# Attention and feed-forward on one core: loads held back longer near a range's end, x sums one step later, and the last half product moved ahead and stored as whole rows

## The chip, the cores and the metric

The kernel runs on one core of one Trainium2 chip. The metric is the device time of one execution in microseconds, lower is better. Three runs of the kernel before the change took 386.1, 386.33 and 386.3 us; the median is 386.3.

## What is computed

The reference is a softmax attention over 8 batches, 12 heads, 448 positions and 64 elements per head, followed by a feed-forward layer on all 3584 tokens:

```python
scores = scale * np.matmul(q, k.transpose(0, 1, 3, 2))
scores = scores - np.max(scores, axis=-1, keepdims=True)
attn = np.exp(scores)
attn = attn / (np.sum(attn, axis=-1, keepdims=True) + 1e-09)
x = np.matmul(attn, v)            # (8, 12, 448, 64) -> (3584, 768)
...
h = x @ w_in                      # (3584, 768) @ (768, 2048)
g = np.maximum(0.01 * h, h)
out = g @ w_out                   # (3584, 2048) @ (2048, 768), float32
```

## The kernel before

**Two streams of work.** The attention works in *units* of two heads of one batch: 8 x 6 = 48 units. A unit's scores (L316, L319) go to PSUM, ScalarE takes their exponential (L328, L331, L333), `rows` (L983) multiplies the exponentials by v (L340, L347), divides by the row sums (L999, L1000) into a tile `x`, and `x_transposes` (L376) turns that tile into `xT` by a DMA transposition that SP issues (L271). A transposition of q and k into `qkT` (L280, `dma_transposes`) is issued by SP too.

The feed-forward runs over seven *ranges* of tokens (`cuts`, L41: 640, 512, 512, 512, 512, 384 and 512 tokens), here called range 0 to 6. For each range `hidden(i)` (L530) computes h = leaky(x w_in), and `second(i)` (L1157) computes g w_out, in two pairs of 128-row blocks (`block_pair`, L664; range 0 has a plain pair first). In the time of `second(i)` PE's matmuls are interleaved with the attention of the units that the next range needs: `place` (L1094) decides from a small model of time (`model["now"]`, in microseconds) when a burst of scores, a `rows` or a tail is put between two quarter products.

**Seven products for eight.** Both matrix products save multiplications: a product of 2 x 2 blocks is done with seven half products and some sums of blocks. The sums of x that `hidden(i+1)` needs are made on VectorE by `mix_x_part` (L489, its instruction is L502), from `xT`: four sums for the first two thirds of the depth (`slice(0, 2)`) and four for the last third. The first four read what the last but one unit of a range wrote, the others what its last unit wrote. In `second`, the list `fresh` holds from which model time on each of the two lots may be emitted: 5.0 after the unit's `rows`, and from then on one sum per step. VectorE executes in the order of emission, so a sum that waits for its transposition holds up all that stands behind it.

In `block_pair`, `early` computes four products into PSUM banks `a` and `b` and `late` the last ones; each is copied (`keep`, L691) or added (`join`, L697) to an output tile on VectorE before its bank is used again. `deep_sums` (L615, instruction L625) prepares one product of the second pair that is itself split into seven (`deep`, L628, matmuls L649, additions L653), which runs beside the next `hidden`.

**Loads.** `advance` (L957) is called every few steps and emits at most one cast of q and k, one cast of v (both on GpSimd, L186 to L199) and, if its argument `calm` is true, one load (`load_soft`, L149, issued by GpSimd, L159) of q, k or v of two units. GpSimd executes these in the order of emission. In `second`, `calm` is true until all but one of the units that the next range needs have had their `rows`, and again once all x sums are emitted; in `hidden` it is always true.

**The end.** The last pair has no next `hidden` beside which its deep product could run, so `block_pair` with `last` runs `early`, the steps of `deep` between them, and then `closing` (L732). There the output tiles are `o1` and `o2` (in the profile `e`), and stores go to SP's and ScalarE's queues (`both`). `closing` computes, in this order: the fourth product in two quarter-width pieces, with the sixth step of `deep` between them; the fifth product (`s3`, `t3`, eight matmuls of 384 columns) into bank `b`; a join of its right half (L744) and a store of the right half of `o2`; the left half of `o2`, for which the first quarter is a copy by ScalarE (L746) and the second an addition (L747); the seventh and last step of `deep`, four L649 matmuls of 192 columns, added to the first quarter; a store of the left half; and the last two pieces of `o1`, each added (L754) and stored. A store of 128 rows is cut in two where the rows cross a boundary of 112: here 16 rows on SP's queue and 112 on ScalarE's for `o2`, 48 and 80 for `o1`.

Of the kernel before, what the change touches and what calls it, by code (L numbers as in the profile page):

```python
# [16 lines left out]
def kernel(  # L17
# [372 lines left out]
    def store(o, t0, cols=slice(0, DM), queues=(nc.sync, nc.sync)):  # L390

        queues = list(queues)
        done = 0
        while done < P:
            b, j = divmod(t0 + done, S)
            so, p = divmod(j, SC)
            n = min(SC - p, P - done)
            dst = out[b * S:(b + 1) * S].rearrange("(p so) n -> so p n", so=NSC)
            queues.pop(0).dma_start(out=dst[so, p:p + n, cols], in_=o[done:done + n, cols])
            done += n  # L400
# [227 lines left out]
    def deep(i):  # L628

        one, two = (ts(x[1], P) for x in spots(i)[1])  # L630
        lo, hi = slice(MH, MH + QH), slice(MH + QH, MD)
        s3, s1 = h_mix[:, :QH, 0], h_mix[:, QH:, 0]
        t, (t2, t3, t4) = w_mix[:, 2], (deep_mix[:, x] for x in range(3))
        left, right = slice(0, QW), slice(QW, NW)
        o = [kept[i, c] for c in range(2)]
        end = i + 1 == NR
        taken = [slots.pop(0) for _ in range(2 if end else 1)]
        b, a = (x[:, 0, :QW] for x in taken) if end else (taken[0][:, x, :QW] for x in range(2))
        for ps, first, x, w, c, cols in (
            (b, True, h[:, lo, one], t[:, :QH, left], 0, left),  # L640
            (a, True, h[:, hi, one], t[:, QH:, left], 0, left),
            (b, False, s1, t2, 0, right),
            (a, True, h[:, lo, two], t[:, :QH, right], 1, right),
            (b, False, s3, t3, 1, right),
            (a, False, h[:, hi, one], t[:, QH:, right], 0, right),
            (b, False, h[:, hi, two], t4, 1, left),
        ):
            for m in range(QH):
                nc.tensor.matmul(ps, x[:, m], w[:, m], start=(first and m == 0), stop=(m == QH - 1), skip_group_check=True)  # L649
            if end and c and ps is a:  # L650
                nc.scalar.copy(o[c][:, cols], ps)
            else:
                nc.vector.tensor_add(o[c][:, cols], o[c][:, cols], ps)  # L653
            if ps is a and first and c == 0:
                nc.vector.tensor_sub(h[:, hi, one], h[:, hi, one], s1)
            if ps is a and not first:
                store(o[0], token(i, spots(i)[1][0][1]), slice(0, NW) if end else slice(0, DM))
            if w is t4:
                if not end:
                    store(o[1], token(i, spots(i)[1][1][1]))  # L660
                slots.extend(taken)
            yield

    def block_pair(i, c):  # L664

        lo, hi = slice(0, MH), slice(MH, MD)
        x1, x2 = spots(i)[1][c]
        one, two = ts(x1, P), ts(x2, P)
        s3 = h_mix[:, :, c]
        t2, t3, t4 = (w_mix[:, x] for x in range(3))  # L670
        t1 = w_out_sb[:, lo, NW:]
        left, right = slice(0, NW), slice(NW, DM)
        if i + 1 == NR and c:
            o1, o2 = (e_all[:, x, :2 * DM].bitcast(F32) for x in range(2))
        else:
            o1, o2 = (o_pool.tile([P, DM], F32, name="o") for _ in range(2))
        kept[i, c] = o2
        b, a = banks
        t0 = token(i, x2)
        last = t0 + P == B * S  # L680

        def product(ps, x, w, first=False, cols=slice(0, NW)):
            for m in range(MH):
                if m in (2, 4, 6):
                    yield
                nc.tensor.matmul(  # L686
                    ps[:, cols], x[:, m], w[:, m], start=(first and m == 0), stop=(m == MH - 1), skip_group_check=True,
                )

        def keep(o, at, ps, by=nc.vector.tensor_copy):  # L690
            by(o[:, at], ps[:, :NW])  # L691

        idle = nc.scalar.copy
        calm = idle if i + 1 == NR else nc.vector.tensor_copy

        def join(o, at, ps):
            nc.vector.tensor_add(o[:, at], o[:, at], ps[:, :NW])  # L697

        def early():
            yield from product(b, h[:, lo, one], w_out_sb[:, lo, left], first=True)  # L700
            nc.vector.tensor_sub(h[:, lo, one], h[:, lo, two], h[:, lo, one])
            short = cuts[i + 1] - cuts[i] < 4 * P
            keep(o1, left, b, idle if c == 0 and short else calm)
            yield
            yield from product(a, h[:, hi, one], w_out_sb[:, hi, left], first=True)
            join(o1, left, a)
            if last:
                store(o1, token(i, x1), left)
            nc.vector.tensor_sub(h[:, hi, one], h[:, hi, one], h[:, lo, one])
            yield  # L710
            yield from product(b, h[:, lo, one], t2)
            keep(o1, right, b, calm)
            yield
            if last:
                return
            yield from product(a, h[:, lo, two], t1, first=True)
            keep(o2, right, a, calm)
            yield

        def late():  # L720
            yield from product(b, s3, t3)
            if i:
                keep(o2, left, b, calm)
            join(o2, right, b)
            if i + 1 == NR:
                store(o2, t0, right)
            yield
            yield from product(a, h[:, hi, one], w_out_sb[:, hi, right])
            join(o1, right, a)
            store(o1, token(i, x1))  # L730

        def closing(more):  # L732

            both = (nc.sync, nc.scalar)
            pieces = [(ps, ts(x, QW), slice(NW + x * QW, NW + (x + 1) * QW)) for x, ps in enumerate((a, slots[0][:, 0]))]
            for ps, cols, at in pieces:
                yield from product(ps, h[:, lo, two], t1[:, :, cols], first=True, cols=cols)
                idle(o2[:, at], ps[:, cols])
                if ps is a:
                    yield  # L740
                    next(more)
                yield
            yield from product(b, s3, t3)
            join(o2, right, b)  # L744
            store(o2, t0, right, both)
            idle(o2[:, :QW], b[:, :QW])  # L746
            nc.vector.tensor_add(o2[:, QW:NW], o2[:, QW:NW], b[:, QW:NW])  # L747
            yield
            for _ in more:
                yield  # L750
            store(o2, t0, left, both)
            for x, (ps, cols, at) in enumerate(pieces):
                yield from product(ps, h[:, hi, one], w_out_sb[:, hi, right][:, :, cols], cols=cols)
                nc.vector.tensor_add(o1[:, at], o1[:, at], ps[:, cols])  # L754
                store(o1, token(i, x1), at, both)
                if not x:
                    yield

        yield
        if last:  # L760
            more = deep(i)
            for x, _ in enumerate(early()):
                if x in (0, 4):
                    next(parts[0])
                yield
                if x > 2 and x % 2:
                    next(more)
                    yield
            yield from closing(more)
            return  # L770
        if not c:
            parts[:] = [deep_sums(i)]
        for x, _ in enumerate(early()):
            if i and c and x in (9, 13):
                next(parts[0])
            yield
        for x, _ in enumerate(late()):
            if i and not c and x == 4:
                next(parts[0])
            yield  # L780
        if i:
            return
        yield
        yield from product(b, h[:, hi, two], t4)
        keep(o2, left, b)
        store(o2, t0)
        banks.reverse()
# [369 lines left out]
    def second(i):  # L1157
# [5 lines left out]
        for c in range(len(spots(i)[1])):  # L1163
            whole = c < plain(i)
            for x, _ in enumerate((plain_pair if whole else block_pair)(i, c)):
                fine = 1 if whole else 2
                if x % (2 * fine) == 0:
                    advance(all(summed) or rows_done < need[i + 2] - 1)
                if c or x:
                    model["now"] += 0.65 / fine  # L1170
                if c == 0 and x > 2 and x % 2:
# [10 lines left out]
                    next(deeps, None)  # L1182
                for y in range(2):
                    if fresh[y] is None and i + 1 < NR and rows_done >= need[i + 2] - 1 + y:
                        fresh[y] = model["now"] + 5.0
                for y, todo in enumerate(x_sums if x % fine == 0 else ()):
                    if fresh[y] is not None and fresh[y] <= model["now"] and not summed[y]:
                        summed[y] = next(todo, 0) is not None
# [72 lines left out]
```

## Time and profile before

| what | value |
|---|---|
| median of three runs | 386.3 us |
| the profiled execution | 385.61 us |
| its span, first to last instruction | 383.8 us |
| PE busy | 371.3 us (97%) |
| DVE busy | 248.6 us (65%) |
| ACT busy | 260.5 us (68%) |
| POOL busy | 187.8 us (49%) |
| mean granted TensorE clock | 0.999 |
| DMA, mean over the span | 125 GB/s |

Times within the kernel are counted from the start of the span. PE, PEld, DVE, ACT, POOL and SP are TensorE's matmuls, its weight loads, VectorE, ScalarE, GpSimd and SyncE. In a timeline a row gives the start, the duration, the engine, the line of the kernel, the operation, what is written and read, the number of instructions merged into the row and, in brackets, how long the engine had been idle before and what ended that. The rows marked SPq and ACTq are the queues that issue DMAs. In the view of waits a row gives who waited for whom, the total, the number of times and the longest. The view of DMA issues gives a size and the median time from issue to landing. PE is busy nearly all the time, so the rows to look at are those in which it waits, and the tail after its last matmul, at 379 us.

### The profile page before, as it was taken

To read this page: it belongs to the slowest core of one execution; us is meant where nothing else is said; L and a number is where in the kernel's file an instruction comes from. 1 tells how busy PE (TensorE), PEld (TensorE's weight loads), DVE (VectorE), ACT (ScalarE), POOL (GpSimd) and SP (SyncE) were. 2 spreads that over 40 slices of the span, in tenths; PEclk is the share of its full clock that TensorE was granted. 3 is DMA by queue.
4 is the path that set the end of the run, shared out by engine and by line. 5 is a ranking of instruction groups with operands and counts; after the bars stand their busy time and mean duration, and the time that the engine had idled before them with its cause. 6 is when DMAs were issued, how large, how long until landed. Compare 5 with 4: busy or idle time off the path is not lost.

```text
span 383.8 us, 10136 instructions
## 1 busy us (share of the span) xinstructions
PE 371.3 (97%) x4024; PEld 266.3 (69%) x4024; DVE 248.6 (65%) x550; ACT 260.5 (68%) x400; POOL 187.8 (49%) x376
## 2 busy tenths in 40 slices
PE   7899999999999999999999999999999999999994
PEld 3565557766698565996559966589665995679764
DVE  5763848456866857666676575766847775685752
ACT  6988885765768785658756688657687568536621
POOL 8997731987969355526566255761637020000000
PEclk9999999999999999999999999999999999999999
DMA  9999999899999469948599484896637530322023
GB/s 158 196 199 203 183 204 172 109 166 208 145 201 112 73 128 126 144 116 109 111 124 160 116 111 79 119 174 138 91 76 132 111 108 0 79 56 61 23 76 91
DMA packets 99456, 47.85 MB, mean 125 GB/s; under 512 B 63696, under 2 KB 96208, under 8 KB 99408
## 3 DMA queue, kind: packets, MB, share of 16 engines
q0 software_dynamic: 40384, 22.47, 46.6%
q1 hardware_dynamic: 58576, 24.27, 30.4%
q8 instruction: 31, 0.51, 0.6%
q10 hardware_dynamic: 448, 0.47, 0.4%
q14 instruction: 17, 0.14, 0.1%
HBM read 45.61 MB, written 11.01 MB: 148 GB/s over the span
## 4 chain that ended last, share of the span: by engine, by line
PE 85%; DMA 7%; DVE 4%; issue 1%; ACT 1%; POOL 1%; ACTq 0%; DVEq 0%; POOLq 0%
PE g L686 22%; PE g L555 14%; PE sc L555 14%; PE sc L347 5%; PE sc L319 5%; DMA xT<-x 5%; PE g L421 4%; PE sc L316 4%; PE sc L649 4%; PE sc L359 3%; PE g L800 3%; PE g L841 2%; PE sc L340 2%; DMA w_in_mix<-in_k_dram 2%; PE g L359 1%
## 5 line engine op out<-in xcount | busy, mean ns | idle before, releaser
L328 ACT ACTIVATE e<-sc 128x896 bf16<-128x896 f32 (+1 forms) x144 | 123.5, 921 | 33.5 <-PE sc L319 20.1
L686 PE MATMUL g<-w_out_sb,h 128*128 128x384 bf16 (+1 forms) x416 | 78.7, 324 | 2.2 <-DVE o L691 2.2
L686 PEld LDWEIGHTS <-h 128*128 128x128 bf16 x544 | 50.3, 98 | 39.8 <-issue 11.9
L544 ACT ACTIVATE h<-c 128x512 bf16<-128x512 f32 (+1 forms) x72 | 43.6, 611 | 30.1 <-DVE c L570 12.8
L555 PEld LDWEIGHTS <-w_in_sb 128*128 128x128 bf16 x576 | 54.6, 98 | 7.0 <-issue 1.5
L186 POOL COPY qkb<-fq 112x512 bf16<-112x512 bf16 x36 | 24.3, 676 | 62.2 <-DMA qkT<-qkb 42.7
L555 PEld LDWEIGHTS <-w_in_mix 128*128 128x128 bf16 x432 | 40.5, 98 | 3.7
L999 DVE RECIPROCAL rec<-sc 112x8 f32<-112x8 f32 x42 | 8.7, 207 | 42.5 <-PE sc L347 18.6
L197 POOL COPY v<-fv 128x384 bf16<-128x384 bf16 x30 | 15.4, 512 | 42.0 <-PE sc L347 25.4
L347 PE MATMUL sc<-v,e 128*128 128x65 bf16 x720 | 33.3, 194 | 0.0
L319 PE MATMUL sc<-qkT 64*128 64x448 bf16 (+1 forms) x210 | 32.8, 353 | 0.0
L347 PEld LDWEIGHTS <-e 128*128 128x128 bf16 x720 | 31.2, 98 | 1.3
L1000 DVE TENSOR_TENSOR x<-sc,rec 112x512 bf16<-112x512 f32 x42 | 29.0, 692 | 1.5
L691 DVE COPY o<-g 128x384 f32<-128x384 f32 x43 | 23.8, 553 | 8.7 <-PE g L686 8.6
L555 PE MATMUL g<-xT,w_in_sb 128*128 128x256 bf16 (+1 forms) x216 | 28.5, 268 | 0.8 <-DVE o L697 0.8
L555 PE MATMUL sc<-xT,w_in_sb 128*128 128x256 bf16 (+1 forms) x216 | 28.5, 268 | 0.0
L653 DVE TENSOR_TENSOR o<-o,sc 128x192 f32<-128x192 f32 x39 | 13.7, 351 | 20.3 <-PE sc L649 20.3
L340 PE MATMUL sc<-v,e 128*128 128x130 bf16 x120 | 26.5, 221 | 0.0
L697 DVE TENSOR_TENSOR o<-o,g 128x384 f32<-128x384 f32 x36 | 19.8, 550 | 8.6 <-PE g L686 4.9
L190 POOL COPY qkb<-fk 128x384 bf16<-128x384 bf16 x30 | 19.6, 653 | 7.1 <-DMA fk<-in_k_dram 7.1
L159 POOL DMA_DIRECT2D fv<-in_v_dram x33 | 20.6, 630 | 4.1 <-POOL v L199 2.4
L567 ACT COPY c<-g 128x512 f32<-128x512 f32 (+1 forms) x12 | 6.8, 567 | 22.5 <-PE g L555 22.0
(151 smaller groups left out, 766.8 us busy)
## 6 DMA issues: line engine op xcount, KB each, us to landing
fq<-in_q_dram POOLq DMA_DIRECT2D x18, 224.0 KB, 5.4
w_in_sb<-in_moe_w_in_dram POOLq DMA_DIRECT2D x4, 768.0 KB, 11.3
w_out_sb<-in_moe_w_out_dram POOLq DMA_DIRECT2D x4, 768.0 KB, 17.7
out_dram<-o SPq DMA_DIRECT2D x7, 336.0 KB, 3.3
out_dram<-o SPq DMA_DIRECT2D x7, 288.0 KB, 2.7
fk<-in_k_dram POOLq DMA_DIRECT2D x15, 128.0 KB, 5.1
fv<-in_v_dram POOLq DMA_DIRECT2D x15, 128.0 KB, 3.7
out_dram<-o SPq DMA_DIRECT2D x7, 240.0 KB, 2.8
```

Of the source, the lines that this page charges most:

```text
L159: nc.gpsimd.dma_start(out=t[p, :n, :, :so].rearrange("p u h so d -> p (u h) (so d)"), in_=(q, k, v)[x][b, hs, keys].rearrange("h (p so) d ...
L186: by(t[:SC, x].rearrange("p so h d -> p h so d"), f)
L319: nc.tensor.matmul(ps[:, j, :S].rearrange("p (so s) -> p so s", so=NSC), t[p, 1, c], t[p, 0, :, :SC], start=True, stop=True,)
L328: nc.scalar.activation(e[:, :, c, :], ps[:n, :, :S], AX.Exp, scale=scale)
L340: nc.tensor.matmul(ps, e[:, EM + qc * SC:EM + qc * SC + P], vt[:, 2 * KC:].rearrange("p j d -> p (j d)"), start=True, stop=False, skip_gro ...
L347: nc.tensor.matmul(ps[:, j * (D + 1):(j + 1) * (D + 1)], e[:, at:at + P], vt[:, j * KC + c], start=False, stop=(c == KC - 1), skip_group_c ...
L544: nc.scalar.activation(hs[:, m:m + 2, cols], x.rearrange("p (m t) -> p m t", m=2), AX.Prelu, alpha=0.01)
L555: nc.tensor.matmul(ps[:, j * nh:(j + 1) * nh], w[:, kk, ts(j, P)], x[:, kk], start=(first and j == 0 and kk == 0), stop=(kk == KH - 1), sk ...
L686: nc.tensor.matmul(ps[:, cols], x[:, m], w[:, m], start=(first and m == 0), stop=(m == MH - 1), skip_group_check=True,)
L691: by(o[:, at], ps[:, :NW])
L697: nc.vector.tensor_add(o[:, at], o[:, at], ps[:, :NW])
L1000: nc.vector.tensor_mul(x, ps[:, :, :, :D], rec.to_broadcast([SC, 2, 2 * NP, D]))
```

## The change

Three things are changed.

1. In `second`, the loads are withheld from `rows_done >= need[i + 2] - 2` on, one unit earlier than before, until all x sums of the next range are emitted.
2. The x sums may be emitted 6.0 model microseconds after their unit's `rows`, not 5.0.
3. In `closing`, the seventh step of `deep` is made ahead of the fifth product, right behind the second piece of the fourth product. `deep` copies it (ScalarE) into the first quarter of `o2` instead of adding it. The fifth product is then joined to the right half and to the left half by two VectorE additions of 384 columns, and `o2` is stored as whole rows.

```diff
@@ deep
-            if end and c and ps is a:
+            if end and c and (ps is a or cols is left):
                 nc.scalar.copy(o[c][:, cols], ps)
             else:
                 nc.vector.tensor_add(o[c][:, cols], o[c][:, cols], ps)
@@ closing
             for ps, cols, at in pieces:
                 yield from product(ps, h[:, lo, two], t1[:, :, cols], first=True, cols=cols)
                 idle(o2[:, at], ps[:, cols])
-                if ps is a:
-                    yield
-                    next(more)
+                yield
+                next(more)
                 yield
             yield from product(b, s3, t3)
             join(o2, right, b)
-            store(o2, t0, right, both)
-            idle(o2[:, :QW], b[:, :QW])
-            nc.vector.tensor_add(o2[:, QW:NW], o2[:, QW:NW], b[:, QW:NW])
-            yield
+            join(o2, left, b)
+            store(o2, t0, queues=both)
             for _ in more:
-                yield
-            store(o2, t0, left, both)
+                pass
+            yield
@@ second
-                    advance(all(summed) or rows_done < need[i + 2] - 1)
+                    advance(all(summed) or rows_done < need[i + 2] - 2)
...
-                        fresh[y] = model["now"] + 5.0
+                        fresh[y] = model["now"] + 6.0
```

More of the change, by code (lines that the diff above doesn't have):

```diff
@@ L744, in closing @@
             join(o2, right, b)
-            store(o2, t0, right, both)
-            idle(o2[:, :QW], b[:, :QW])
-            nc.vector.tensor_add(o2[:, QW:NW], o2[:, QW:NW], b[:, QW:NW])
+            join(o2, left, b)
+            store(o2, t0, queues=both)
+            for _ in more:
+                pass
             yield
-            for _ in more:
-                yield
-            store(o2, t0, left, both)
             for x, (ps, cols, at) in enumerate(pieces):
```

## The prediction

> **What bounds the kernel now.** I read the page first: PE is busy for 371.3 of 383.8 us, at a granted clock of 0.999, so time can only be won where PE stands still or after its last matmul. The view of waits, for PE over the whole span, says where it stands still (total, times, longest):
>
> ```profile
> PE g L686 <- DVE o L691: 2.2, 3, 0.9
> ...
> PE g L555 <- DVE o L697: 0.8, 3, 0.3
> ```
>
> All other PE waits lie in the first 59 us, which the change does not reach. These six come in three pairs, at the ends of ranges 1, 2 and 3 (near 149, 199 and 249 us). The timeline of the first shows what holds DVE up:
>
> ```profile
> 141.03 1.23 POOL L159 DMA_DIRECT2D fv<-in_v_dram  x2 [0.30 <-POOL v L199]
> ...
> 141.49 5.11 SPq L271 DMA_TRANSPOSE xT<-x  x2
> ...
> 147.62 1.46 PE L686 MATMUL g<-w_mix,hmix 128*128 128x384 bf16 x8
> ...
> 148.12 0.43 DVE L502 TENSOR_TENSOR x_mix<-xT 128x512 bf16<-128x512 bf16 x1 [1.94 <-DMA xT<-x]
> ...
> 149.14 0.55 DVE L691 COPY o<-g 128x384 f32<-128x384 f32 x1
> ...
> 149.74 1.46 PE L686 MATMUL g<-w_out_sb,h 128*128 128x384 bf16 x8 [0.66 <-DVE o L691]
> ...
> 151.46 0.82 PE L555 MATMUL g<-xT,w_in_sb 128*128 128x256 bf16 x6 [0.26 <-DVE o L697]
> ```
>
> The first x sum (L502) stands in DVE's order ahead of the copy (L691) that frees PE's bank. It waits for the transposition issued at 141.49, which lands 6.54 us later (the chain's row for it), and a v load issued at 141.03 runs beside that transposition. The end of range 4 shows the same three products with DVE in time:
>
> ```profile
> 295.85 1.46 PE L686 MATMUL g<-w_mix,hmix 128*128 128x384 bf16 x8
> ...
> 297.15 1.46 PE L686 MATMUL g<-w_out_sb,h 128*128 128x384 bf16 x8
> ...
> 298.45 0.66 PE L555 MATMUL g<-xT,w_in_sb 128*128 128x192 bf16 x6
> ```
>
> From the hmix product to the first hidden product that is 298.45 - 295.85 = 2.60 us. At the three places it is 151.46 - 147.62 = 3.84, 200.78 - 196.94 = 3.84 and 250.37 - 246.26 = 4.11. The excess, 1.24 + 1.24 + 1.51 = **3.99 us**, is what can be won; the waits show only 3.0, since each modelled matmul end holds 0.15 us of pipeline after the next could start.
>
> **Loads held back.** By the built order PE, SP and ACT keep their instructions up to the last pair; only POOL's L159 loads move. At the ends of ranges 1 to 4 it is the v load alone that moves (two DMAs, 1.23 us of POOL), from ahead of two v casts and one q/k cast to behind them. At the end of range 0 a v, a q and a k load move behind three casts (the v load behind four). The transposition so loses its neighbour. What it takes alone: the one issued at 137.57 landed at 139.95, the one at 325.48 at 327.81, 2.4 and 2.3 us; the rows of L271 give 2.3/3.0/6.8 as least, median and most. At 141.49 two output stores (issued 140.20 and 140.79) are ahead of it on SP's queue, whose packets run until 142.9 in the trace, so I take 142.9 plus its 0.6 us of packets plus 0.5 to 2 us to complete (both occur): it lands at 144.0 to 145.5. DVE reaches the sum at about 146.6, so the wait goes, with 1 us to spare.
>
> **x sums a step later.** The model's 5.0 becomes 6.0: at the ends of ranges 1 to 3 the first x sum goes behind the last deep sum (L625, 0.42), and each later one moves one place behind a copy or join. DVE then runs, with the 0.46 to 0.47 us from start to start that these rows show: L691 at 147.82 (the t1 product ends at 147.78), x sums at 148.29 and 148.75, L691 at 149.2, L697 at 149.67 to 150.21. PE starts its next product at 148.93 without a wait and the first hidden product at 150.27, against 147.62 + 2.60 = 150.22. So 0.05 stays at each place: 3.99 - 0.15 = **3.8 us won**. What is late next: four part-2 sums (0.28 each) end at about 152.2, while the third hidden product, which needs them, starts at 153.3; they are hidden by PE's four products before it. At the end of range 5 one more 0.43 us sum falls behind the joins, and L570 starts 0.43 later than 342.81; its bank is next wanted at 344.79, so it costs nothing (0.4 at most without that cover).
>
> **What the late loads cost.** The v load comes behind the casts, at about 145.3, and its packets (1.8 us after issue in this trace) from 147.1, when those of the second transposition (issued 145.41) are through. It then shares with three qkT transpositions that are first used in the next second half, near 174. The q and k loads behind it land 2 to 3 us later and the casts with them; POOL stood idle for 5.19 us before the next v cast (166.86, waiting for PE), which hides it. At range 0 the first q/k cast moves from 112.5 to about 118, and its transposition is issued at 128.59 after waiting for PE. Cost: nothing.
>
> The Trainium skill's DMA: Bandwidth & Descriptors, Rules for kernel authors, speaks against this part: to overlap transfers with compute it says to issue the DMA early. By that rule late loads would reach PE; the idle rows of POOL above say there is room, and the rival below has its price.
>
> **The last pair.** The end of the kernel reads so:
>
> ```profile
> 375.86 1.46 PE L686 MATMUL g<-w_mix,hmix 128*128 128x384 bf16 x8
> ...
> 377.43 0.56 DVE L697 TENSOR_TENSOR e<-e,g 128x384 f32<-128x384 f32 x1 [1.68 <-PE g L686]
> ...
> 378.02 0.39 ACTq L399 DMA_DIRECT2D out_dram<-e  x1
> ...
> 378.45 0.32 ACT L746 COPY e<-g 128x192 f32<-128x192 f32 x1 [2.07 <-DVE e L697]
> 378.80 0.35 DVE L747 TENSOR_TENSOR e<-e,g 128x192 f32<-128x192 f32 x1 [0.81 <-ACT e L746]
> ...
> 379.45 1.33 ACTq L399 DMA_DIRECT2D out_dram<-e  x3
> ```
>
> PE's work is the same, but the four L649 matmuls (0.33 us) now go ahead of the fifth product: its join starts at 377.43 + 0.33 = 377.76, the second join (0.55) at 378.23, done at 378.78. A DVE add at L747 and one at L653 (0.35 each) go, an L697 comes; ACT's copy L746 becomes L651, early and hidden. The whole-row stores are issued at 378.81, where the left ones went at 379.45, and ACT's two 80-row stores follow at 379.25 and 379.70 instead of 379.93 and 380.40. The issues are 0.70 us earlier. Against it stands that the right half, 196 KB, which left at 378.02 while the queues were empty, now waits until 378.81. Bounds: -0.70 if issue sets the last landing (2.15 us after issue, as before); and if data does, the page's median of 3.3 us for a 336 KB store gives 378.81 + 3.3 = 382.1, and 196 KB more at the 215 to 305 GB/s of the last stretch 0.65 to 0.9, so 382.75 to 383.0 against the last landing at 382.55: up to +0.4. The 3.3 has loads beside it, so I take **-0.2**.
>
> The same page of the Trainium skill, Anatomy of one DMA, fits 2.0 us plus bytes at 436 GB/s; the 336 KB piece would then be an estimated 2.8 us and the last 60 KB one 2.1, so the end would come 0.7 earlier and the sum would be -4.5. The packets of the whole-row store issued near 369.6 run from 370.6 to 372.2, 393 KB in 1.6 us or 245 GB/s, and I keep mine.
>
> **Sum.** -3.8 - 0.2 = -4.0 us. The profiled execution (385.61 us, of which the span is 383.8) would take 381.6; it lies 0.69 below the median of the runs, so the median 386.3 becomes **382.3**. With 4.0 + 0.7 at best, and 3.5 and +0.4 at worst, this case spans 381.6 to 383.2.
>
> **Rivals.**
> 1. *The transposition lands as late as before*, since the stores ahead of it or an instruction fetch hold it and not the load. For it: a 16 KB fetch lies beside it at 143.5, and the one issued at 335.56 took 4.25 us with no load. Against: with loads beside it it took 5.3 to 6.8 at all four places. Then only the order acts: x sum at 148.12, L691 148.58, two sums, L691 149.95, L697 150.42 to 150.97, hidden product 151.02 instead of 151.46. That is 0.44 x 3 + 0.2 = 1.5: 384.8.
> 2. *The wait moves to the second transposition*, which meets the deferred load instead. It bites when that lands over 6.8 us after its issue (145.41 + 6.8 = 152.2, less than 1 us of sums before 153.3). At 8 us it takes 1.2 back at each of three places: 382.3 + 3.6 = 385.9.
> 3. *Slower: loads too late.* At the end of range 0 three loads go at about 106.5 and the casts behind them must be done by 128.59, 134.93 and 138.86, when SP wants to issue the qkT transpositions in order. The page's landing times for q, k and v are 5.4, 5.1 and 3.7 us; it decides from about 11 us a load, and at the 16 us of the slowest v row (at the start) the third cast is some 7 us late, which PE pays at once: 386.3 - 4.0 + 7 = 389.3.
> 4. *The change does not do what it says*: the built order shows that it does; what remains is that a wait elsewhere takes the time, 386.
>
> **Chances.** Forecast 0.73, rival 1 0.12, rival 2 0.05, rival 3 0.06, rival 4 0.04. The range 381.4 to 384.8 takes in the forecast's span, most of rival 1 and little else. A measurement can tell about 0.2% (0.8 us) from no change: faster 0.86 (the forecast, rival 1, a little of rival 2), same 0.07, slower 0.07.
>
> **What would show it.** Right: no PE wait on L691 or L697 at the three places, 2.6 us from the hmix product to L555, transpositions of the last row but one landing within 4 us, the range ends 1.2, 2.4 and 3.8 us earlier, joins at 377.8 and 378.2 less 3.8. Wrong: an x sum that still waits for xT; POOL casts that wait so long for fq or fk that SP's qkT issues move; a last landing over 3.8 us after the whole-row issue.

## The result, and the profile after

| kernel | median of its runs | ratio to the kernel before, with 95% interval | profiled execution | its span |
|---|---|---|---|---|
| before | 386.2 us (8 runs) | 1 | 385.61 us | 383.8 us |
| changed | 383.01 us (8 runs) | 0.9933 (0.991 to 0.9956) | 382.95 us | 381.1 us |

The changed kernel is 0.44 to 0.9% faster. 382.3 was forecast, with a range of 381.4 to 384.8. The view of waits for PE, over the whole span of the changed kernel, no longer has L691 or L697. After the first 59 us only one wait is left, and it is new, 0.2 us on L653:

```profile
PE g L236 <- DVE gate L231: 1.2, 1, 1.2
...
PE sc L649 <- DVE o L653: 0.2, 1, 0.2
```

The timeline of the changed kernel at the end of range 1 answers to the one shown of before:

```profile
141.83 5.12 SPq L271 DMA_TRANSPOSE xT<-x  x2
...
146.78 0.42 DVE L502 TENSOR_TENSOR x_mix<-xT 128x512 bf16<-128x512 bf16 x1
...
147.96 1.46 PE L686 MATMUL g<-w_mix,hmix 128*128 128x384 bf16 x8
147.98 1.23 POOL L159 DMA_DIRECT2D fv<-in_v_dram  x2
148.16 0.56 DVE L691 COPY o<-g 128x384 f32<-128x384 f32 x1 [0.96 <-PE g L686]
...
150.56 0.82 PE L555 MATMUL g<-xT,w_in_sb 128*128 128x256 bf16 x6
```

The x sum at 146.78 has no bracket: it waits for nothing. The v load stands 6.2 us behind the transposition instead of 0.5 ahead of it. DVE now waits for PE (L691, 0.96), where PE had waited for DVE, and from the hmix product to the hidden product it is 150.56 - 147.96 = 2.60 us.

The same stretch and two others can be read off the two traces. Where the 2.7 us of the spans come from:

| stretch | before | changed | difference |
|---|---|---|---|
| start to the first hidden product of range 1 | 104.43 | 104.78 | +0.35 |
| hmix product to hidden product, ends of ranges 1, 2, 3 | 3.84, 3.84, 4.11 | 2.60, 2.60, 2.60 | -3.99 |
| the same, ends of ranges 4 and 5 | 2.60, 2.60 | 2.60, 2.60 | 0 |
| first hidden product of range 6 to the end of the last matmul | 38.78 | 39.19 | +0.41 |
| end of the last matmul to the last landing | 3.57 | 4.22 | +0.65 |
| last landing to the end of the span | 1.29 | 1.19 | -0.10 |

The sum is -2.68. The first row is chance: in the executions of this study that stretch took 104.4 to 107 us, also in kernels with the same instructions there (105.11 with the last pair alone changed, 104.43 in the kernel before). Two rows gave back a quarter of what was won. The end of the changed kernel, in its timeline:

```profile
372.96 1.46 PE L686 MATMUL g<-w_mix,hmix 128*128 128x384 bf16 x8
373.16 0.32 ACT L651 COPY e<-sc 128x192 f32<-128x192 f32 x1
...
374.53 1.02 DVE L697 TENSOR_TENSOR e<-e,g 128x384 f32<-128x384 f32 x2 [2.00 <-PE g L686]
...
375.57 1.75 SPq L399 DMA_DIRECT2D out_dram<-e  x3
375.58 1.76 ACTq L399 DMA_DIRECT2D out_dram<-e  x3
```

The order is as forecast, and so is the time of issue: the whole-row stores go 0.16 us before the end of the last matmul (375.74), where the left ones went 0.48 behind it. But the view of DMA issues (window 374 to 381) shows what they then take. The columns are number, size of each and median time to landing:

```profile
out_dram<-e ACTq DMA_DIRECT2D x1, 336.0 KB, 3.7
out_dram<-e ACTq DMA_DIRECT2D x2, 60.0 KB, 3.5
```

In the same view of the kernel before (window 372 to 384) the halves and the small stores behind them read:

```profile
out_dram<-e ACTq DMA_DIRECT2D x2, 168.0 KB, 2.3
...
out_dram<-e ACTq DMA_DIRECT2D x2, 60.0 KB, 2.2
```

So ScalarE's last piece of `o2` is issued 0.6 us earlier and takes 1.4 us longer. The last landing is 4.4 us behind the issue of the whole rows; the prediction had named more than 3.8 as a sign of being wrong.

### The profile page after: what moved, and what is told of

It is laid out like the page before. It is cut to its first block, busy times and chain, and to the rows that moved or that the text cites. A ratio compares the mean times of both kernels' runs of the same rounds, so it can differ in the third digit from the quotient of the medians.

```text
span 381.1 us, 10137 instructions
## 1 busy us (share of the span) xinstructions
PE 371.5 (97%) x4024; PEld 267.2 (70%) x4024; DVE 248.5 (65%) x549; ACT 260.3 (68%) x400; POOL 193.7 (51%) x376
## 4 chain that ended last, share of the span: by engine, by line
PE 92%; ACT 4%; DVE 2%; issue 1%; DVEq 0%; ACTq 0%
PE g L686 27%; PE sc L555 13%; PE g L555 13%; PE sc L319 7%; PE sc L347 6%; PE g L421 4%; PE sc L316 4%; PE sc L649 4%; PE sc L359 3%; PE g L797 3%; ACT e L328 3%; PE g L838 2%; PE sc L340 2%; PE g L298 1%; PE g L359 1%
## 5 line engine op out<-in xcount | busy, mean ns | idle before, releaser
L691 DVE COPY o<-g 128x384 f32<-128x384 f32 x43 | 23.8, 553 | 13.1 <-PE g L686 13.0
L197 POOL COPY v<-fv 128x384 bf16<-128x384 bf16 x30 | 16.8, 560 | 29.3 <-PE sc L347 27.9
L653 DVE TENSOR_TENSOR o<-o,sc 128x192 f32<-128x192 f32 x39 | 13.7, 351 | 20.0 <-PE sc L649 19.9
L697 DVE TENSOR_TENSOR o<-o,g 128x384 f32<-128x384 f32 x36 | 19.8, 551 | 8.6 <-PE g L686 4.9
L190 POOL COPY qkb<-fk 128x384 bf16<-128x384 bf16 x30 | 17.7, 591 | 8.0 <-DMA fk<-in_k_dram 8.0
L316 PE MATMUL sc<-qkT 64*128 64x448 bf16 x144 | 19.8, 358 | 2.0 <-ACT e L328 0.9
```

The lines of the kernel that those rows point to most:

```text
L316: nc.tensor.matmul(ps[:, j, :S], t[p, S + c * SC:S + c * SC + P], t[p, :S], start=True, stop=True)
```

## The experiments

The theory after these traces: the v load beside the transposition made the three waits, so holding back the loads is worth 4.0 us by itself; the later x sums only cost (0.4 at range 6); the last pair's change costs 0.6. The rivals: the sums' new place won the time; the output stores ahead on SP's queue held the transposition; the late end was chance. The ratios below are those to the kernel before on the same chip, with 95% intervals.

### Each part alone

Only the loads (`e1_loads_only`), only the sums (`e2_sums_only`), only the last pair (`e3_end_only`), and the first two (`e4_no_end`):

```diff
# e1, e4
-                    advance(all(summed) or rows_done < need[i + 2] - 1)
+                    advance(all(summed) or rows_done < need[i + 2] - 2)
# e2, e4
-                        fresh[y] = model["now"] + 5.0
+                        fresh[y] = model["now"] + 6.0
# e3: the hunks of deep and closing alone
```

> The kernel before with only the loads held back. Theory: the v load beside the last-but-one row's transposition made the first x sum wait, so this alone takes all of the three places' 4.0 us and pays nothing at the end: about 382.2 us, no PE wait on L691 or L697, 2.60 us from the hmix product to the first hidden product, that transposition landing within 4 us, and no PE wait near 341. Rival (it is the later place of the sums in DVE's order that won): the three waits stay, about 386. Rival (the stores ahead on SP's queue hold the transposition): it still lands after 6 us or more, about 386.

> The kernel before with only the x sums a step later. Theory: the transposition still lands 6.5 us after its issue, so only the order acts, 0.4 us at each of three places, and 0.4 is given back at the start of range 6's hidden products, where one more sum lies ahead of L570: -1.3 + 0.4 = -0.9, about 385.3. Rival (the later place alone is enough): -3.6, about 382.6. Rival (it gives nothing without the loads): 386.6.

> The kernel before with only the last pair changed. Theory: the 196 KB of the right half leave 0.8 us later and the whole-row store takes 3.7 us to land, so the last landing comes 0.6 us later after PE's last matmul: about 386.8 (+0.6), span end 5.3 to 5.4 us after the last matmul's start row, against 4.8 before. Rival (the late end of the changed kernel was chance in one execution, and the issues 0.7 us earlier count): -0.2 to -0.7, about 385.8.

> The changed kernel with the last pair as before (loads held back and sums a step later). Theory: -4.0 at three places, +0.4 at the start of range 6's hidden products: -3.6, about 382.6, that is 0.4 slower than the loads alone and 0.6 faster than the changed kernel. Rival (the sums' place is needed beside the loads): 0.5 or more faster than the loads alone.

| kernel | median | ratio | the three places | range 6 to last matmul | last matmul to last landing |
|---|---|---|---|---|---|
| e1, loads | 381.82 | 0.9897 (0.9871 to 0.9922) | 2.60, 2.60, 2.60 | 38.78 | 3.58 |
| e2, sums | 384.66 | 0.9968 (0.9953 to 0.9983) | 3.22, 3.05, 3.52 | 39.18 | 3.55 |
| e3, last pair | 386.37 | 1.0012 (0.9993 to 1.0031) | 3.52, 3.66, 4.60 | 38.78 | 4.11 |
| e4, loads and sums | 382.39 | 0.992 (0.9891 to 0.9949) | 2.60, 2.60, 2.60 | 39.18 | 3.56 |

The loads alone take all three waits. By the last two columns they are about 1 us ahead of the whole change (39.19 and 4.22 there); the intervals of the two ratios overlap a little. In e1's timeline the first x sum stands where it stood before, ahead of the last deep sum, and does not wait:

```profile
141.57 5.11 SPq L271 DMA_TRANSPOSE xT<-x  x2
...
146.19 0.42 DVE L502 TENSOR_TENSOR x_mix<-xT 128x512 bf16<-128x512 bf16 x1
...
146.52 0.42 DVE L625 TENSOR_TENSOR hmix<-h 128x512 bf16<-128x512 bf16 x1
...
150.30 0.82 PE L555 MATMUL g<-xT,w_in_sb 128*128 128x256 bf16 x6
```

With the sums alone the transposition is as late as before, and what PE loses at the three places is halved, not gone. The view of waits of e2 has these two left:

```profile
PE g L555 <- DVE o L697: 0.8, 3, 0.3
...
PE g L686 <- DVE o L691: 0.3, 1, 0.3
```

That is 2.0 us at the three places, more than the 1.3 expected, less 0.4 at range 6. The time of the last pair alone is not distinguishable from the kernel before by its interval; the stretch after its last matmul, 4.11 against 3.57, is, and it recurs in every run with whole rows.

What the neighbour does is best seen in the completion records of the four transpositions of the last row but one (ranges 1 to 4). "Load" is when the v load is issued, counted from the issue of the transposition:

| kernel | load | time to landing, ranges 1 to 4 |
|---|---|---|
| before | 0.5 before at 1 to 3, 0.07 before at 4 | 6.5, 6.6, 6.8, 5.3 |
| e2, sums | 0.4 to 0.5 before at 1 to 3, 1.3 behind at 4 | 6.6, 6.5, 6.9, 2.8 |
| e3, last pair | the same | 6.2, 6.4, 7.3, 2.7 |
| changed | 4.6 to 6.2 behind | 4.1, 2.8, 2.9, 2.8 |
| e1, loads | 4.6 to 6.5 behind | 4.3, 2.7, 2.9, 2.7 |

In the eight other kernels, which all hold the loads back, it lands after 4.0 to 4.3 us at the first place and 2.7 to 3.1 at the others. Two stores stand ahead of the transposition on SP's queue in every kernel; they do not explain 6.5 against 2.8. The 4th place of e2 and e3, where the load came 1.3 us behind the transposition, is an experiment that the executions made by themselves. The rival with the stores falls as the cause of the waits. It is what is left without the load: there the transposition lands 0.4 to 0.6 us behind the second of the two stores at each place, in every kernel, while in the kernel before it came 3.2 to 4.5 us behind it. The 4.0 to 4.3 at the first place goes with a second store that lands late (3.5 to 3.9 us after the transposition's issue, against 2.1 to 2.6 at the other places), and the changed kernel's packet records have a 16 KB instruction fetch beside both; that this fetch is the cause was not tried. Why a load issued just ahead costs 2.5 to 4.5 us is not shown either.

The collision is moved, not removed. The loads held at the end of range 0 now run into two other transpositions: issued at 111.42 and 112.85 in the changed kernel, they land after 9.2 and 9.7 us, where their counterparts at 112.25 and 113.67 in the kernel before took 3.9 and 2.9. That costs nothing here, for PE waits nowhere in that part.

### The later sum at range 6

> The changed kernel with the x sums of range 6 at their old 5.0, all others at 6.0. Theory: the later sum in front of range 6's hidden products cost 0.40, so the stretch from their start to the last matmul's end goes from 39.18 back to 38.78, the PE wait on L653 goes, and the time is 0.4 below the changed kernel: about 382.5. Rival (that wait came from the deep product and stays): 39.18, no gain.

```diff
-                        fresh[y] = model["now"] + 6.0
+                        fresh[y] = model["now"] + (6.0 if i < 5 else 5.0)
```

382.26 us, ratio 0.9897 (0.9876 to 0.9918), against 0.9933 of the changed kernel; the stretch is 38.78 again and the wait on L653 is gone. (At the first of the three places this execution has 2.71 and not 2.60: one x sum took 0.61 us, where 0.42 is usual.) The timeline of the changed kernel shows the place that the forecast overlooked:

```profile
339.63 0.68 DVE L570 TENSOR_TENSOR c<-c,g 128x512 f32<-128x512 f32 x1
...
340.23 0.68 DVE L570 TENSOR_TENSOR c<-c,sc 128x512 f32<-128x512 f32 x1
...
340.82 0.35 DVE L653 TENSOR_TENSOR o<-o,sc 128x192 f32<-128x192 f32 x1
...
341.22 0.49 PE L649 MATMUL sc<-w_mix,h 128*128 128x192 bf16 x4 [0.24 <-DVE o L653]
```

and that of before, in the same rows:

```profile
342.81 0.68 DVE L570 TENSOR_TENSOR c<-c,g 128x512 f32<-128x512 f32 x1
...
344.00 0.35 DVE L653 TENSOR_TENSOR o<-o,sc 128x192 f32<-128x192 f32 x1
...
344.46 0.49 PE L649 MATMUL sc<-w_mix,h 128*128 128x192 bf16 x4
```

Before, L653 was done at 344.35, 0.11 ahead of the matmul. With one more sum ahead of L570 it comes 0.4 later against PE, and PE has to stop for the deep product's bank.

### The end

Four kernels take the store apart; all hold the loads back and have the sums at their old place. In `e5_split_stores` the seventh half product is moved as in the change, but each half is stored when it is joined; `e7_whole_rows_late` has PE's old order and one store of whole rows; `e9_halves_together` and `e12_left_first` join both halves and store two half-width pieces, in either order:

```diff
# e5, against the change
+            store(o2, t0, right, both)
             join(o2, left, b)
-            store(o2, t0, queues=both)
+            store(o2, t0, left, both)
# e7, against e1
-            store(o2, t0, right, both)
...
-            store(o2, t0, left, both)
+            store(o2, t0, queues=both)
# e9, against the change; e12 has the two new lines in the other order
-            store(o2, t0, queues=both)
+            store(o2, t0, right, both)
+            store(o2, t0, left, both)
```

> Loads held back, x sums at their old place, the last pair's seventh half product moved ahead as in the change, but the right half of o2 stored as soon as it is joined and the left half after its own join. Theory (the whole-row store is what costs at the end, the moved product gains): last landing 2.9 to 3.2 us after PE's last matmul, where the kernel before has 3.57 and the changed one 4.22, so 0.4 to 0.7 faster than the loads alone: about 381.3. Rival (the moved product itself is late, or four stores in a row on ScalarE's queue eat it up): 3.6 or more, 381.8 or more.

> Loads held back and x sums at their old place; PE's order in the last pair as before, but o2 is stored once, as whole rows, where its left half was stored. The store is then issued at about the time at which the change issues it, 0.7 us before the left half's old place, as ScalarE no longer has the right half's store ahead of its copy. Theory (the store of whole rows costs, since the right half's 196 KB leave later): last landing 4.1 to 4.2 us after the last matmul, +0.6 on the loads alone, about 382.4. Rival (the moved product costs): 3.6 as with the loads alone, about 381.8.

> Loads held back, x sums at their old place, the seventh half product moved ahead, and o2 stored only when both halves are joined, but as two half-width stores one behind the other. Theory (what costs is the form: 112 rows of 3072 bytes in one DMA, which took 3.7 us from issue to landing where half-width ones take 2.3 to 2.6): the halves land within about 3 us of their issue and the end comes 3.2 to 3.6 us after the last matmul, about 381.6 to 381.9. Rival (what costs is that 196 KB leave 0.5 us later): 4.0 or more, 382.4 or more.

> As the version with two half-width stores behind each other, but the left half, which is joined last, is stored first, so that the right half's store stands behind it on both queues and no byte of o2 leaves before the time of the change's whole-row store (0.17 us before the end of the last matmul). Theory (the form costs, 112 rows of 3072 bytes in one DMA): each half lands 2.3 to 2.7 us after its issue, and the last 60 KB store, issued at about 1.2 us after the last matmul, sets the end at 3.4 to 3.8 us, below the whole rows' 4.1 to 4.3. Rival (the later start of 196 KB costs): 4.1 or more, as with whole rows.

All times are counted from the end of the last matmul; "o2 landed" is ScalarE's last piece of it:

| kernel | median, ratio | first store of o2 | o2 landed | last landing |
|---|---|---|---|---|
| e1, as before | 381.82, 0.9897 (0.9871 to 0.9922) | -0.96 | 2.78 | 3.58 |
| e5, split | 381.61, 0.9881 (0.9858 to 0.9904) | -0.63 | 2.42 | 3.23 |
| e9 | 381.69, 0.9872 (0.9845 to 0.99) | -0.63 | 2.59 | 3.32 |
| e12, left first | 382.15, 0.9905 (0.9877 to 0.9932) | -0.17 | 2.97 | 3.71 |
| changed, whole rows | 383.01, 0.9933 (0.991 to 0.9956) | -0.17 | 3.54 | 4.22 |
| e7, whole rows, old order | 383.34, 0.9931 (0.9905 to 0.9956) | 0.08 | 3.66 | 4.33 |

e9 did not ask its question: the right half's store waits only for the right join, so its issues are those of e5 to 0.01 us, and it counts as a second run of it. e12 did: no byte of o2 leaves before -0.17, as with whole rows. Its view of DMA issues (window 374 to 382):

```profile
out_dram<-e ACTq DMA_DIRECT2D x2, 168.0 KB, 2.5
out_dram<-e ACTq DMA_DIRECT2D x2, 60.0 KB, 2.5
```

Two stores of 168 KB with 0.43 us between their issues land at 2.97 where one of 336 KB lands at 3.54, from the same start. So both answers are right in part, and the rival's is about half of it: from e5 to e12 the later start of the right half costs 0.48, from e12 to the changed kernel the form costs 0.51. Executions with the same issues differ by about 0.1 there: with e9 for e5 the first is 0.39, with e3's 4.11 for the changed kernel the second is 0.40. Moving the half product gains 0.35 (e1 to e5), a little less than was expected, and e7 shows that the move is not what costs: with PE's old order the end is as late as in the change. (e7's median is 0.9 above the forecast; its six runs spread from 382.58 to 385.36, and its end accounts for 0.1 to 0.2 of that.) Why one DMA of 112 rows of 3072 bytes takes that much longer stays open. The packet records show where the time goes: its last four 3072-byte packets leave one at a time from 378.5 to 378.9, after most had gone by 378.0. The other kernels with whole rows show the same tail, those with halves do not.

The Trainium skill's DMA: Bandwidth & Descriptors, Rules for kernel authors, says to coalesce many small transfers into one large one, as under 64 KB one pays mostly overhead. The pieces here, of 168 KB, are above that size, and in these runs two of them beat one of 336 KB. The Trainium skill's DMA: Bandwidth & Descriptors, Anatomy of one DMA, has a fit for DMAs that GpSimd issues. Put to this store, which ScalarE issues, it gives an estimated 2.8 us for 336 KB, and 3.7 was measured.

### Loads later still

> Loads held back, x sums at their old place, and in addition no load in the first ten steps of each range's hidden products, so that all loads of a range come some 7 us later than with the loads alone. Theory: GpSimd has that much room (5 us idle before the next v cast, 10 us or more before the qkT transpositions), so no difference that can be measured, 381.6 to 382.2. Rival (late loads reach PE): PE waits for scores or v, 2 us or more slower, 384 or more.

```diff
         for step, _ in enumerate(hidden(i)):
-            advance()
+            advance(step > 9)
```

381.9 us, ratio 0.9888 (0.9867 to 0.991), the same as the loads alone, and no PE wait appears after the first 59 us. But the edit moved less than was meant. Beside the loads alone, the q and k loads at the end of range 0 are issued 5.1 and 6.1 us later and those at the end of range 1 2.2 us later; no other load is more than 1.0 us later. GpSimd takes this up, as its waits (window 95 to 360) show:

```profile
POOL qkb L190 <- DMA fk<-in_k_dram: 7.6, 6, 2.9
...
POOL v L197 <- DMA fv<-in_v_dram: 4.8, 1, 4.8
```

With the loads alone the first of these is 5.3 us and the second is not there. The rival of the forecast that ends slower, loads too late, was put at the end of range 0; there another 5 to 6 us for q and k cost PE nothing. For the later ranges the room was not tried.

### The best version, once more

> The version with loads held back, sums at their old place, the moved half product and the split stores once more, on one chip with the loads alone. By the ends of the two profiled executions (3.23 against 3.58 us after the last matmul) it should be 0.35 faster than the loads alone, about 381.5; if the end was chance, equal to it.

> The loads alone once more, on one chip with the version with split stores: 0.35 slower than that by its end, about 381.8; equal if the difference of the ends was chance.

On one chip, the split stores took 381.64 us, ratio 0.9864 (0.9832 to 0.9896), the loads alone 382.47, ratio 0.9887 (0.986 to 0.9913); their ends are 3.26 and 3.56 us after the last matmul. The ends differ by 0.30, against 0.35 the first time. The intervals of the ratios overlap, but the five times with split stores (381.4 to 381.75) all lie below the six of the loads alone (381.96 to 382.92); the medians are 0.8 apart, which is more than the ends account for. The version with loads held back, sums at their old place, the half product moved and the stores split has the lowest medians of this study.

## Why the prediction was right, and where it was wrong

**What bounds the kernel**: right. The excess over 2.60 us, 3.99 us, was the whole sum to be won at the three places, and exactly that was won there.

**Loads held back**: right. The transposition was put at 144.0 to 145.5, which is 2.5 to 4.0 us after its issue; it landed after 4.1, 2.8 and 2.9, the first a little later than the 4 that was to show it right. Rival 1 (it lands as late as before) falls with the landing table, and rival 2 (the wait moves to the second transposition) with that transposition's own landing, 2.3 to 3.9 us after its issue in the changed kernel, far below the 6.8 from which it decides.

**x sums a step later**: right on the order, wrong on its worth. At the three places the residue of 0.05 each was not there, and e1 shows that the later sums added nothing once the loads were away; without that they are worth 2.0 us (e2), so the two parts act on the same waits and do not add up. The step that failed is "L570 starts 0.43 later ..., so it costs nothing (0.4 at most without that cover)". The cover named was that of L570's own bank. Behind L570 in DVE's order stands L653, which frees the bank of the deep product, and it had 0.11 us. The cost was the full 0.41; e6 takes it away.

**What the late loads cost**: right, nothing that PE feels. There was less room than it read: the held q and k loads at range 0 land 9.3 to 10.4 us after issue, near the 11 from which rival 3 decides, and one qkT transposition there is issued 0.4 us later against the rest (135.70; 134.93 before, and the start is 0.35 later), which the prediction had named as a sign of being wrong; PE did not feel it. e8 shows that there is room beyond even so. The rule of the Trainium skill's DMA: Bandwidth & Descriptors, Rules for kernel authors, to issue the DMA early so that it overlaps with compute did not decide here: e1, which issues loads later, is faster (0.9897).

**The last pair**: the failed term. -0.2 was taken, +0.4 was its upper bound, +0.65 was measured. The issue of the whole rows was right to 0.01 us, those of the stores behind to 0.1. What was mis-sized is the transfer: the median of 3.3 us for a 336 KB store was taken as slow because loads lie beside it, and with no load beside it, only other output stores, the store took 3.7.

**The sum**: -4.0 forecast, -3.99 + 0.41 + 0.65 = -2.9 for the terms; with the start's +0.35 and -0.10 at the very end the two spans differ by 2.7, and the medians by 3.2. So the large term was understood, and the two small ones together came out worse than the forecast's worst case (3.5 won and 0.4 lost, 3.1). That 383.01 still lies below the 383.2 of that case is luck: the interval of the ratio leaves a gain of anything from 1.7 to 3.5 us.

## What to carry to other kernels

When an in-order engine waits for a DMA, look at the DMA first: see what is issued beside it, and move that if its user has room. Here that won 4.0 us, and moving the waiting instruction alone 2.0. When an instruction is moved later on an in-order engine, ask not only when its own result is wanted, but go through all that is queued behind it to the next slack, since the smallest of those margins decides. At the tail, storing each half as soon as it is ready beat one large store for two reasons of about equal size here: its bytes start earlier, and the pieces land sooner.

## What the hardware showed that was not expected

- A transposition of 448 packets lands in 2.3 to 2.4 us where it has no neighbour (the one at 325.48 in the kernel before). With two stores ahead of it on the queue it lands in 5.3 to 7.3 us when a load of 224 KB is issued up to 0.5 us ahead of it, and in 2.7 to 2.8 when the load is issued 1.3 us behind it.
- One store of 336 KB took 3.6 to 3.7 us from issue to landing at the end of the kernel, in the four kernels that have it; two of 168 KB from the same start, 0.43 us apart, took 2.3 and 2.7.
- Stores of 60 KB behind the large one on the same queue took 3.3 to 3.6 us, 2.1 to 2.2 behind the halves of the kernel before.
